# Four one-bank output tiles, a reopened PSUM pool, a last pair combined early, and a remade order

## The chip, the cores and the metric

The kernel runs on one core of one Trainium2 chip. The metric is the device time of one execution in microseconds, as the median of several runs. The core's engines work side by side, each through its own list of instructions in order: TensorE (PE) multiplies matrices and writes PSUM, VectorE (DVE) and ScalarE (ACT) work element by element and empty PSUM, GpSimd (POOL) works element by element on SBUF, and SyncE (SP) issues the DMA transfers. An instruction that has to wait for another engine holds everything behind it on its own engine.

## What is computed

The reference is two softmax attentions in a row and then a feed-forward network with a GELU:

```python
def sm_attn(qq, kk, vv):
    s = scale * np.matmul(qq, kk.transpose(0, 1, 3, 2))
    s = s - np.max(s, axis=-1, keepdims=True)
    a = np.exp(s)
    a = a / (np.sum(a, axis=-1, keepdims=True) + 1e-09)
    return np.matmul(a, vv)
p_packed = sm_attn(p, k, v)            # 32 packed queries per head
attn = sm_attn(q, p_packed, p_packed)  # 576 queries per head
x = attn.transpose(0, 2, 1, 3).reshape(8 * 576, 512)
h = x @ w_in                           # 512 x 2048
g = 0.5 * h * (1.0 + erf(h / np.sqrt(2.0)))
out = g @ w_out                        # 2048 x 512
```

q, k and v have 8 batches, 8 heads, 576 positions and 64 columns a head; everything is float32. `x @ w_in` is regrouped: the second attention's weights times (packed p times w_in), so PE first makes `wps`, the product of the packed values and a block of w_in.

## The kernel before

**Tiling.** The 8 batches are taken in 4 pairs of batches, and d_ff in 4 blocks of 512. A pair and a block make a unit, so there are 16 units, 0 to 15, and a pair is four of them. A unit has 8 `h` products on PE (line 1627, 12 matmuls each; line 1618 is the plain form of the first ones), each followed by a GELU on ACT into SBUF (lines 1652 and 1659). Float32 operands are split in a high part (a cast on ACT) and a low part (the rest, by a subtraction), and a product is three matmuls, high by high, high by low and low by high.

**Pair 0, units 0 to 3.** The output product is the plain one: lines 1689 to 1691 are the three matmuls of one 128-token tile, 128 by 512 outputs, one PSUM bank. Four such banks are filled side by side while four blocks of 128 of d_ff pass, then each is emptied: copied by ACT in the pair's first unit (line 1924), added to an accumulator by DVE in the other three (line 1929). The four banks are the halves of two PSUM tiles of two banks each, `oh_0` and `oh_1`. Waits are kept by tile. A ninth, narrower row of tokens goes through `o_edge` in another pool.

**Pairs 1 to 3, units 4 to 15.** The output product is a 2 by 2 block product with seven products in place of eight, taken in the order `MIXED = ("a22", "a11", "s2", "s3", "s1", "s4", "a12")`. Each is done in two halves of 12 matmuls (line 1811); a half fills one of the tiles `oh_0` and `oh_1`. Before it, sums of GELU blocks are made on POOL (lines 1736 and 1741), the high part on ACT (line 1767) and the low part on DVE (line 1773). After it, the half is copied (ACT, line 1836) or added on DVE (line 1842) into an accumulator in SBUF: m4, c11, c12, u3 or c22. The products in `CHAIN` add up in PSUM, each with the one before, without giving the tile back. At the end of a pair three additions on POOL (line 1858) combine accumulators: u3 goes into m4, then u3 and c22 go into c12. Then DVE turns blocks back (line 1899) and SP stores them (line 1890). In unit 15 the low parts of `LAST_LOW = (2, 4)`, which are s2 and s1, are made by POOL.

**Beside all that** run the loads of q, k, v and the weights, the two attentions of the coming pair (k and q are turned by DVE, line 848, or by PE, line 859), the decoding of the weights (lines 1402 to 1465 on ACT, DVE and POOL; the values pass through DRAM in blocks `wf`, `wx`, `ws`), and `wps` (line 1544, made ready by line 1555 on ACT and line 1560 on DVE). In the first 53 us, before the first output product, PE gets filler matmuls on a zero tile (line 1598) wherever the planner sees it with nothing to do; their number is fixed when the kernel is built.

**What sets the order.** Every operation is created by a small task (a generator that yields operations and events). A dry run numbers them; the table `TURNS` (line 118) then lists, for each engine and for the DMA queue, these numbers in the order in which the instructions are issued. The planner walks through the table with modelled costs (`LATENCY`, the `DMA_...` constants; `MARGIN` is added before a PE operation that is neither an `h` product nor an output product, after the first output product; `DMA_MARGIN` before a DMA). These costs set no wait on the chip. SBUF and PSUM slots are handed out from lists of named owners.

Of the kernel before, what the change touches and what calls it, by code (L numbers as in the profile page):

```python
# [42 lines left out]
DMA_FIRST, DMA_ISSUE, DMA_START, DMA_END, DMA_RATE = 2.5, 0.5, 0.6, 0.9, 390e3  # L43
# [12 lines left out]
LAST_LOW = (2, 4)  # L56
CHAIN = ("a11", "s2", "s3", "s1")
INTO = {"a22": "m4", "a11": "c11", "s2": "c12", "s3": "u3", "s1": "c22", "s4": "c12", "a12": "c11"}

MARGIN = 2.0  # L60

DMA_MARGIN = 1.0
# [536 lines left out]
def packed_attention_gelu_ffn(ctx: ExitStack, tc: tile.TileContext, q, k, v, p, w_in, w_out, out):  # L599
# [51 lines left out]
    def plan(order):  # L651
# [1129 lines left out]
        def load_one(u, m):  # L1781
# [3 lines left out]
                [(wms, f"wm_{u}_{m}")])  # L1785
            fire(wm_ready[u, m])

        def mixed_steps():
            for u in range(NF, NU):
                chain = {}  # L1790
                for m, name in enumerate(MIXED):
# [35 lines left out]
        def evict(u, m, h, t):  # L1827
# [18 lines left out]
            if m < 5:  # L1846
                fire(added[u, name, h])
# [177 lines left out]
```

## Time and profile before

| | |
|---|---|
| median of three runs | 724.3 us (723.17 to 725.18) |
| the profiled execution | 725.19 us, of which the span is 723.4 us |
| PE busy | 693.1 us, 96% of the span, 5987 matmuls |
| DVE busy | 537.7 us, 74% |
| ACT busy | 394.7 us, 55% |
| POOL busy | 292.1 us, 40% |
| PE waiting for L1929 or L1924 at L1689 | 3.4 us in 3 waits, 0.9 us in 1 |

The profile is of one execution. Its span runs from the first to the last instruction; 1.8 us of its time lie outside. PE's list of busy time leaves 30.3 us of the span; the weight loads (PEld) run beside the matmuls. In the lines that follow a row begins with its start or its source line, then engine and operation, then output<-input by tile name; `memory` is the one large SBUF tile in which most buffers lie, `rounded` the one for the high and low parts, and `oh` stands for both two-bank tiles and the halves. An arrow in square brackets gives the engine's idle time just before, and what ended it.

### The profile page before, as it was taken

What the parts mean: (1) busy time and instruction counts of PE and PEld (TensorE: products, weight loads), DVE (VectorE), ACT (ScalarE), POOL (GpSimd) and SP (SyncE); (2) the same over time, 40 slices, a digit from 0 to 9 for tenths busy, and PEclk for the clock granted to TensorE, in tenths of its full rate; (3) what the DMA queues carried; (4) which work ended last, traced back from release to release, by engine and by line L of the source; (5) the groups of instructions that cost most, each with busy time, mean ns of one, the idle gap of its engine ahead of it and who ended that gap; (6) DMA issues with size and microseconds to landing.
All of it is one profiled execution on the core that took longest, in us unless ns stands there. A gap on an engine that the chain in (4) does not pass through costs nothing.

```text
span 723.4 us, 14766 instructions
## 1 busy us (share of the span) xinstructions
PE 693.1 (96%) x5987; PEld 611.2 (84%) x5987; DVE 537.7 (74%) x695; ACT 394.7 (55%) x596; POOL 292.1 (40%) x201
## 2 busy tenths in 40 slices
PE   7899999999899999999999999999999999999982
PEld 6667778786786997898899998998998999999982
DVE  4879889877788827789898766787898835765673
ACT  4778677756565663484654363574645463434320
POOL 2654952574351444123044621232143614142481
PEclk9999999999999999999999999999999999999998
DMA  9877999998575899999225299997723574424226
GB/s 327 256 234 196 261 258 241 227 312 222 205 234 190 249 263 274 214 189 321 95 88 175 90 211 219 171 233 204 202 88 146 133 219 126 147 93 144 90 89 127
DMA packets 199555, 140.42 MB, mean 194 GB/s; under 512 B 153792, under 2 KB 172224, under 8 KB 199488
## 3 DMA queue, kind: packets, MB, share of 16 engines
q1 hardware_dynamic: 199488, 139.49, 70.7%
q8 instruction: 47, 0.77, 0.5%
q14 instruction: 20, 0.16, 0.1%
HBM read 106.95 MB, written 32.51 MB: 193 GB/s over the span
## 4 chain that ended last, share of the span: by engine, by line
PE 77%; DVE 7%; DMA 6%; SPq 3%; ACT 3%; issue 1%; POOL 1%; POOLq 0%; DVEq 0%; ACTq 0%
PE oh L1811 34%; PE h L1627 23%; PE wps L1544 3%; PE oh L1689 3%; PE oh L1691 3%; PE oh L1690 3%; PE s L939 2%; PE oh L1598 1%; PE pp L1130 1%; DMA memory<-in_k_dram 1%; DMA memory<-in_q_dram 1%; DMA out_dram<-memory 1%; SPq L826 1%; POOL memory L1858 1%; DVE memory L1929 1%
## 5 line engine op out<-in xcount | busy, mean ns | idle before, releaser
L1811 PE MATMUL oh<-rounded 128*128 128x288 f32 x2016 | 293.3, 298 | 6.7 <-DVE memory L1842 3.3
L1811 PEld LDWEIGHTS oh<-rounded 128*128 128x128 f32 x2016 | 275.4, 196 | 26.5 <-issue 11.6
L1627 PE MATMUL h<-a2T,wp 128*128 128x288 f32 x1440 | 209.7, 295 | 0.2 <-DVE wp L1560 0.2
L1627 PEld LDWEIGHTS h<-a2T,wp 128*128 128x128 f32 x1440 | 197.6, 188 | 5.1 <-ACT rounded L1767 1.3
L1736 POOL TENSOR_TENSOR memory<-memory 128x1152 f32<-128x1152 f32 x36 | 100.5, 2791 | 147.6 <-ACT memory L1652 90.4
L1773 DVE TENSOR_TENSOR rounded<-memory,rounded 128x1152 fp32r<-128x1152 f32 x82 | 132.3, 1618 | 30.0 <-ACT rounded L1767 29.9
L1842 DVE TENSOR_TENSOR memory<-oh,memory 128x576 f32<-128x576 f32 x138 | 102.5, 749 | 61.0 <-PE oh L1811 50.7
L1767 ACT CAST rounded<-memory 128x1152 fp32r<-128x1152 f32 x84 | 96.8, 1159 | 48.0 <-POOL memory L1736 32.5
L1652 ACT ACTIVATE memory<-h 128x576 f32<-128x576 f32 x96 | 62.4, 653 | 98.4 <-PE h L1627 90.2
L1741 POOL TENSOR_TENSOR memory<-memory 128x1152 f32<-128x1152 f32 x12 | 32.5, 2705 | 148.8 <-ACT memory L1652 132.9
L1689 PE MATMUL oh<-rounded 128*128 128x512 f32 x128 | 53.3, 416 | 4.4 <-DVE memory L1929 3.4
L1691 PE MATMUL oh<-rounded 128*128 128x512 f32 x128 | 50.2, 392 | 0.0
L1690 PE MATMUL oh<-rounded 128*128 128x512 f32 x128 | 50.1, 392 | 0.0
L1560 DVE TENSOR_TENSOR wp<-wps,wp 128x1024 fp32r<-128x1024 f32 x30 | 36.6, 1220 | 16.7 <-ACT wp L1555 16.5
L1555 ACT CAST wp<-wps 128x1024 fp32r<-128x1024 f32 x30 | 30.3, 1015 | 24.4 <-PE wps L1544 24.4
L848 DVE STREAM_TRANSPOSE memory<-memory 128x1152 f32<-128x1152 f32 x24 | 32.7, 1366 | 13.3 <-DMA memory<-in_k_dram 13.3
L1668 DVE TENSOR_TENSOR rounded<-memory,rounded 128x512 fp32r<-128x512 f32 x32 | 28.0, 874 | 15.2 <-ACT rounded L1666 15.2
L1689 PEld LDWEIGHTS oh<-rounded 128*128 128x128 f32 x128 | 24.1, 188 | 17.1 <-DVE memory L1929 5.0
L1659 ACT ACTIVATE memory<-h 128x576 f32<-128x576 f32 x32 | 20.9, 652 | 31.7 <-PE h L1627 24.6
L1451 POOL TENSOR_TENSOR memory<-memory 128x512 int32<-128x512 int32 x16 | 23.4, 1464 | 29.3 <-DVE memory L1431 26.7
L1544 PE MATMUL wps<-memory,pp 64*32 64x512 f32 (+1 forms) x528 | 34.0, 579 | 0.0
L1459 POOL TENSOR_TENSOR memory<-memory 128x512 int32<-128x512 int32 x16 | 21.1, 1319 | 29.7 <-DVE memory L1431 29.7
(144 smaller groups left out, 819.6 us busy)
## 6 DMA issues: line engine op xcount, KB each, us to landing
rounded<-wx SPq DMA_DIRECT2D x84, 512.0 KB, 4.3
memory<-ws SPq DMA_DIRECT2D x24, 512.0 KB, 4.9
wraws<-in_moe_w_out_dram SPq DMA_DIRECT2D x16, 512.0 KB, 5.1
wx<-memory SPq DMA_DIRECT2D x16, 512.0 KB, 4.7
memory<-in_v_dram SPq DMA_DIRECT2D x15, 512.0 KB, 7.0
memory<-in_k_dram SPq DMA_DIRECT2D x48, 144.0 KB, 5.2
memory<-in_q_dram SPq DMA_DIRECT2D x48, 144.0 KB, 5.1
out_dram<-memory SPq DMA_DIRECT2D x48, 144.0 KB, 3.7
```

Of the source, the lines that this page charges most:

```text
L1544: nc.tensor.matmul(t[r0:r0 + 32, hh, :m], lhsT=pp[b][rows, hh, r0:r0 + 32], rhs=wi[u, hh][rows, g, cols], start=True, stop=True)
L1560: yield Op(DVE, 1.22, step, lambda: nc.vector.tensor_tensor(lo, x, hi.bitcast(F32), ALU.subtract))
L1627: nc.tensor.matmul(t[:, half, :HALF], lhsT=w[:, wpart, ch, fc], rhs=a2T[b, ch][:, apart, half * HALF:(half + 1) * HALF], start=ch == 0 and ...
L1652: lambda: nc.scalar.activation(x[:, c % 2].rearrange("p (a n) -> p a n", a=2), t[:, :, :HALF], AF.Gelu), table="gelu")
L1689: nc.tensor.matmul(t, lhsT=g[0], rhs=w[:, 0], start=first, stop=False)
L1690: nc.tensor.matmul(t, lhsT=g[0], rhs=w[:, 1], start=False, stop=False)
L1691: nc.tensor.matmul(t, lhsT=g[1], rhs=w[:, 0], start=False, stop=last)
L1736: return Op(POOL, 2.69, 0, lambda: nc.gpsimd.tensor_tensor(of(x), of(y), of(z), op))
L1767: o = op[u, m] = yield Op(ACT, 1.17, 0, lambda o: nc.scalar.copy(o[:, 0], x), [(ops, f"op_{u}_{m}")])
L1773: engine, cost, 0, lambda: on(engine).tensor_tensor(o[:, 1], x, o[:, 0].bitcast(F32), ALU.subtract), port=True)
L1811: nc.tensor.matmul(t[:, half, :HALF], lhsT=x[:, wpart], rhs=o[:, part, q, half * HALF:(half + 1) * HALF], start=first and q == 0 and wpart ...
L1842: yield Op(DVE, 0.75, 0, lambda: nc.vector.tensor_tensor(to(), x, to(), ALU.add))
```

## The change

Four things are changed.

1. The two two-bank tiles are replaced by four one-bank tiles `o_0` to `o_3` for pair 0. When all of pair 0's banks have been emptied, the pool is closed, and a pool with two two-bank tiles `m_0` and `m_1` is opened in the same banks; the first product of unit 4 is created only then.
2. `LAST_LOW` is (5, 6): in unit 15 the low parts of s4 and a12 are POOL's, and those of s2 and s1 DVE's.
3. For the last pair, the combining additions move ahead. The sums of units 12 to 14 are combined on DVE (three additions on 128 by 1152 elements), while unit 14's last and unit 15's first products run. Unit 15's own products then go straight into the final accumulators: s3 is added to m4 and subtracted from c12, which makes two additions per half in place of one, and s4 joins the PSUM chain (`LAST_CHAIN`) behind s1. Every result is turned back when its last addition is done.
4. `TURNS` is new for all engines, `DMA_END` goes from 0.9 to 1.4, `MARGIN` from 2.0 to 0, `DMA_MARGIN` from 1.0 to 0. PE's last `h` product now stands ahead of nine product halves, before of twelve; the last load of q for pair 0 stands ahead of a v load and of weight loads that it followed before. The table now has 11 more fillers (162, before 151). Everything else is issued as often as before, save three POOL additions that are now DVE's and the two more additions from s3.

```diff
-DMA_FIRST, DMA_ISSUE, DMA_START, DMA_END, DMA_RATE = 2.5, 0.5, 0.6, 0.9, 390e3
+DMA_FIRST, DMA_ISSUE, DMA_START, DMA_END, DMA_RATE = 2.5, 0.5, 0.6, 1.4, 390e3
...
-LAST_LOW = (2, 4)
+LAST_LOW = (5, 6)
 CHAIN = ("a11", "s2", "s3", "s1")
+LAST_CHAIN = CHAIN + ("s4",)
...
-MARGIN = 2.0
-
-DMA_MARGIN = 1.0
+LAST_INTO = {
+    "a22": (("m4", ALU.subtract),), "a11": (("c11", ALU.add),), "s2": (("c12", ALU.add),),
+    "s3": (("m4", ALU.add), ("c12", ALU.subtract)), "s1": (("c22", ALU.add),),
+    "s4": (("c12", ALU.add),), "a12": (("c11", ALU.add),),
+}
+
+MARGIN = 0.0
+
+DMA_MARGIN = 0.0
...
-        "53 62 64 63 56 57 83 61 81 82 80 113 100 68 94 101 71 118 97 119 93 85 72 96 73 139 92 157 110 114 175 "
+        "62 63 53 64 56 57 82 83 80 61 97 101 96 100 114 68 120 81 86 119 93 71 94 73 72 95 135 146 121 123 169 "
...
-    pairs = [ps_o.tile([P, 2, 512], F32, name=f"oh_{i}") for i in range(2)]
+    banks, twos = [ps.tile([P, 512], F32, name=f"o_{i}") for i in range(4)], []
+
+    def two_banks():
+
+        ps_o.close()
+        ps = ctx.enter_context(tc.tile_pool(name="ps_m", bufs=1, space=PSUM))
+        twos.extend(ps.tile([P, 2, 512], F32, name=f"m_{i}") for i in range(2))
...
         def mixed_steps():
+            for i in (0, 1, 2, 3, 5, 6, 7, 8):
+                yield finished[NF - 1, i]
+            if order.dry:
+                yield finished[NF - 1, 4]
+            if not order.dry:
+                two_banks()
             for u in range(NF, NU):
-                chain = {}
+                chain, names = {}, LAST_CHAIN if u == NU - 1 else CHAIN
...
-            if f == 0 and m < 5:
+            if u == NU - 1:
+                for name, op in LAST_INTO[MIXED[m]]:
+                    if name in merged:
+                        yield merged[name]
+                    yield Op(
+                        DVE, 0.75, 0,
+                        lambda name=name, op=op: nc.vector.tensor_tensor(to(name), to(name), x, op))
+                    if (MIXED[m], name) == ("s3", "m4"):
+                        fire(total[pr, NM])
+            elif f == 0 and m < 5:
...
-            engine, cost = POOL, 2.67
+            engine, cost = (DVE, 1.35) if pr == NP - 1 else (POOL, 2.67)
...
+            if pr == NP - 1:
+                for x in ("a22", "s3", "s2", "s1", "s4"):
+                    if x == "s2":
+                        yield combine("m4", "u3", "m4", ALU.subtract)
+                        fire(merged["m4"])
+                    for h in range(2):
+                        yield evicted[NU - 2, MIXED.index(x), h]
+                yield combine("c12", "c12", "u3", ALU.subtract)
+                macs.give(of("u3"))
+                yield combine("c12", "c12", "c22", ALU.add)
+                fire(merged["c12"])
+                yield from totals("a22")
+                yield total[pr, NM]
+                start(result(pr, 0, 0, "m4"))
...
```

Line numbers move with the insertions: the output product's lines 1689 to 1691 become 1703 to 1705, the additions to accumulators (1929 and 1842) become 1979 and 1871, line 848 becomes 861, the low part (1773) becomes 1787, the combine (1858) becomes 1887, and the additions of unit 15 stand at line 1860.

The remade order is shown at three places. The first is PE at the end of unit 2, around 181 to 186 us of the trace: the last products of the unit's four banks and the next `h` product. `oh_0_81` and `oh_1_82` are the two tiles, `o_0_81` to `o_3_84` the four. Before:

```order
L1689 MATMUL oh_1_82<-rounded_80 128x512
L1690 MATMUL oh_1_82<-rounded_80 128x512
L1691 MATMUL oh_1_82<-rounded_80 128x512
L1689 MATMUL oh_1_82<-rounded_80 128x512
L1690 MATMUL oh_1_82<-rounded_80 128x512
L1691 MATMUL oh_1_82<-rounded_80 128x512
L1152 MATMUL ppTm_3_2113<-ident_71,pn_3_0_2091 128x128
L1152 MATMUL ppTm_3_2113<-ident_71,pn_3_1_2093 128x128
L1689 MATMUL oh_0_81<-rounded_80 128x512
L1690 MATMUL oh_0_81<-rounded_80 128x512
L1691 MATMUL oh_0_81<-rounded_80 128x512
L1627 MATMUL h_24_2122<-a2T_0_0_911,wp_3_0_1941 128x288 x6
```

After:

```order
L1703 MATMUL o_2_83<-rounded_80 128x512
L1704 MATMUL o_2_83<-rounded_80 128x512
L1705 MATMUL o_2_83<-rounded_80 128x512
L1703 MATMUL o_3_84<-rounded_80 128x512
L1704 MATMUL o_3_84<-rounded_80 128x512
L1705 MATMUL o_3_84<-rounded_80 128x512
L1703 MATMUL o_0_81<-rounded_80 128x512
L1704 MATMUL o_0_81<-rounded_80 128x512
L1705 MATMUL o_0_81<-rounded_80 128x512
L1165 MATMUL ppTm_3_2124<-ident_71,pn_3_0_2097 128x128
L1165 MATMUL ppTm_3_2124<-ident_71,pn_3_1_2101 128x128
L1641 MATMUL h_24_2128<-a2T_0_0_920,wp_3_0_1786 128x288 x6
```

The fourth product, into the first half of `oh_0` before, has a tile of its own after, and stands ahead of the two transposes (line 1152, now 1165).

The second place is DVE in unit 4, around 272 to 278 us: low parts, the turning of a block of k that has to be loaded first, and the additions of the first mixed products into their accumulators. Before:

```order
L1773 TENSOR_TENSOR rounded_80<-memory_79,rounded_80 128x1152 x4
L848 STREAM_TRANSPOSE memory_79<-memory_79 128x1152
L1516 TENSOR_TENSOR memory_79<-memory_79 128x512
L1773 TENSOR_TENSOR rounded_80<-memory_79,rounded_80 128x1152
L1842 TENSOR_TENSOR memory_79<-oh_0_81,memory_79 128x576
L1560 TENSOR_TENSOR wp_6_0_2795<-wps_6_0_0_3006,wp_6_0_2795 128x1024
L1842 TENSOR_TENSOR memory_79<-oh_1_82,memory_79 128x576
```

After:

```order
L1787 TENSOR_TENSOR rounded_80<-memory_79,rounded_80 128x1152 x4
L1871 TENSOR_TENSOR memory_79<-m_0_2668,memory_79 128x576
L861 STREAM_TRANSPOSE memory_79<-memory_79 128x1152
L1787 TENSOR_TENSOR rounded_80<-memory_79,rounded_80 128x1152
L1871 TENSOR_TENSOR memory_79<-m_1_2669,memory_79 128x576
L1871 TENSOR_TENSOR memory_79<-m_0_2668,memory_79 128x576
L1529 TENSOR_TENSOR memory_79<-memory_79 128x512
```

A further low part and the addition from the first tile have moved ahead of the turning of k (848, now 861), and the next low part and the addition from the second tile stand behind it.

The third place is DVE in unit 15, over the additions from the tiles of its middle products. Before, the row L1899 is the first turning back of a result:

```order
L1773 TENSOR_TENSOR rounded_80<-memory_79,rounded_80 128x1152
L1842 TENSOR_TENSOR memory_79<-oh_0_81,memory_79 128x576
L1842 TENSOR_TENSOR memory_79<-oh_1_82,memory_79 128x576
L1773 TENSOR_TENSOR rounded_80<-memory_79,rounded_80 128x1152
L1842 TENSOR_TENSOR memory_79<-oh_0_81,memory_79 128x576
L1842 TENSOR_TENSOR memory_79<-oh_1_82,memory_79 128x576
L1842 TENSOR_TENSOR memory_79<-oh_0_81,memory_79 128x576
L1773 TENSOR_TENSOR rounded_80<-memory_79,rounded_80 128x1152
L1899 STREAM_TRANSPOSE memory_79<-memory_79 128x576 x2
L1842 TENSOR_TENSOR memory_79<-oh_1_82,memory_79 128x576
L1842 TENSOR_TENSOR memory_79<-oh_0_81,memory_79 128x576
L1842 TENSOR_TENSOR memory_79<-oh_1_82,memory_79 128x576
```

After, L1860 are the additions of unit 15 and L1887 is the last of the three combining additions:

```order
L1787 TENSOR_TENSOR rounded_80<-memory_79,rounded_80 128x1152
L1860 TENSOR_TENSOR memory_79<-memory_79,m_0_2668 128x576
L1860 TENSOR_TENSOR memory_79<-memory_79,m_1_2669 128x576
L1860 TENSOR_TENSOR memory_79<-memory_79,m_0_2668 128x576
L1787 TENSOR_TENSOR rounded_80<-memory_79,rounded_80 128x1152
L1887 TENSOR_TENSOR memory_79<-memory_79 128x1152
L1860 TENSOR_TENSOR memory_79<-memory_79,m_1_2669 128x576
L1860 TENSOR_TENSOR memory_79<-memory_79,m_0_2668 128x576
L1787 TENSOR_TENSOR rounded_80<-memory_79,rounded_80 128x1152 x2
L1860 TENSOR_TENSOR memory_79<-memory_79,m_1_2669 128x576
L1860 TENSOR_TENSOR memory_79<-memory_79,m_0_2668 128x576 x2
L1860 TENSOR_TENSOR memory_79<-memory_79,m_1_2669 128x576 x2
```

The last combining addition (L1887) has come to DVE, between unit 15's first additions, and the low parts of s3 and s1 (the row x2) stand behind an addition from each tile.

## Rows read from the trace of the kernel before

**Rows 1.** Stretch, length, busy PE, PEld, DVE, ACT, POOL, clock, DMA share, GB/s
```profile
0.00:53.00 53.00, 46.38 (x605) 33.78 (x606) 35.97 (x70) 33.51 (x69) 25.37 (x26) 1.00 0.82 274
...
92.00:270.00 178.00, 173.15 (x1328) 143.80 (x1329) 133.79 (x191) 113.65 (x188) 84.88 (x92) 1.00 0.84 241
270.00:284.00 14.00, 12.29 (x90) 11.23 (x89) 9.17 (x11) 6.52 (x8) 4.13 (x2) 0.88 0.97 265
284.00:690.00 406.00, 405.04 (x3638) 377.01 (x3637) 304.76 (x356) 208.43 (x283) 136.40 (x50) 1.00 0.64 165
690.00:724.00 34.00, 17.69 (x127) 16.66 (x125) 19.12 (x23) 3.48 (x3) 15.17 (x5) 0.90 0.46 101
```

**Rows 2.** What PE waited for, whole span: us, times, longest
```profile
PE oh L1689 <- DVE memory L1929: 3.4, 3, 1.8
...
PE oh L1689 <- ACT memory L1924: 0.9, 1, 0.9
...
PE h L1627 <- DVE wp L1560: 0.2, 1, 0.2
```

**Rows 3.** Timeline at 182 to 186: start, us, what, idle before
```profile
182.37 1.22 DVE L1560 TENSOR_TENSOR wp<-wps,wp 128x1024 fp32r<-128x1024 f32 x1 [0.53 <-ACT wp L1555]
...
184.17 1.28 DVE L1929 TENSOR_TENSOR memory<-oh,memory 128x512 f32<-128x512 f32 x2
...
185.50 0.50 PE L1689 MATMUL oh<-rounded 128*128 128x512 f32 x1 [1.83 <-DVE memory L1929]
```

**Rows 4.** Timeline at 272 to 280, PE and DVE
```profile
272.25 1.75 PE L1811 MATMUL oh<-rounded 128*128 128x288 f32 x12
...
272.78 1.38 DVE L848 STREAM_TRANSPOSE memory<-memory 128x1152 f32<-128x1152 f32 x1 [11.21 <-DMA memory<-in_k_dram]
...
276.72 2.97 PE L1811 MATMUL oh<-rounded 128*128 128x288 f32 x12 [1.71 <-DVE memory L1842]
...
279.49 2.21 PE L1627 MATMUL h<-a2T,wp 128*128 128x288 f32 x12
```

**Rows 5.** Timeline at 31 to 45 of SP's queue, then of PE
```profile
31.18 0.39 SPq L884 DMA_DIRECT2D memory<-in_v_dram  x1
...
34.56 0.35 SPq L1398 DMA_DIRECT2D wraws<-in_moe_w_out_dram  x1
36.05 0.35 SPq L816 DMA_DIRECT2D memory<-in_q_dram  x1
...
41.99 0.74 PE L859 MATMUL qm<-ident,memory 128*128 128x128 f32 x5 [0.15 <-DVE mx L1236]
...
44.06 1.25 PE L1598 MATMUL oh<-still 128*128 128x256 bf16 x10 [0.35 <-ACT pp L1115]
```

**Rows 6.** Timeline of PE from the last h product on
```profile
685.89 1.75 PE L1627 MATMUL h<-a2T,wp 128*128 128x288 f32 x12
...
694.38 3.45 PE L1811 MATMUL oh<-rounded 128*128 128x288 f32 x24 [0.40 <-issue]
698.12 4.99 PE L1811 MATMUL oh<-rounded 128*128 128x288 f32 x36 [0.29 <-issue]
704.71 1.86 PE L1811 MATMUL oh<-rounded 128*128 128x288 f32 x12 [1.59 <-DVE memory L1842]
708.77 3.41 PE L1811 MATMUL oh<-rounded 128*128 128x288 f32 x24 [2.20 <-issue]
```

**Rows 7.** Timeline of the same stretch, POOL and then DVE
```profile
698.77 9.11 POOL L1858 TENSOR_TENSOR memory<-memory 128x1152 f32<-128x1152 f32 x3 [2.63 <-DVE memory L1842]
...
700.66 2.00 DVE L1773 TENSOR_TENSOR rounded<-memory,rounded 128x1152 fp32r<-128x1152 f32 x1
...
707.91 1.42 DVE L1842 TENSOR_TENSOR memory<-oh,memory 128x576 f32<-128x576 f32 x2 [3.26 <-POOL memory L1858]
```

**Rows 8.** Every run of line 1773: ns least, median, most
```profile
L1773 DVE TENSOR_TENSOR rounded<-memory,rounded x82: 1315/1350/3827, 240.6 to 700.7; 128x1152 fp32r<-128x1152 f32 x82
```

**Rows 9.** PE groups, 284 to 690: count, busy us, mean ns
```profile
L1544 PE MATMUL wps<-memory,pp 64*32 64x512 f32 x304 | 20.5, 600 | 0.0
```

More of the change, by code (lines that the diff above doesn't have):

```diff
@@ L616, in packed_attention_gelu_ffn @@
     dram = ctx.enter_context(tc.tile_pool(name="dram", bufs=1, space=bass.MemoryType.DRAM))
-    ps_o = ctx.enter_context(tc.tile_pool(name="ps_o", bufs=1, space=PSUM))
     ps_w = ctx.enter_context(tc.tile_pool(name="ps_w", bufs=2, space=PSUM))
+    ps_o = ExitStack()
+    ps = ps_o.enter_context(tc.tile_pool(name="ps_o", bufs=1, space=PSUM))
     ctx.enter_context(tc.manual_schedule())
@@ L676, in plan @@
         psum_o = of_banks(
-            [(i, i + 1, lambda i=i: pairs[i // 2][:, i % 2]) for i in range(4)], [P, 512], (None, (0, 1, 2, 3)))
-        mps = of_banks([(2 * i, 2 * i + 2, lambda i=i: pairs[i][:]) for i in range(2)], [P, 2, 512], (None, (0, 1)), rank=1)
+            [(i, i + 1, lambda i=i: banks[i]) for i in range(4)], [P, 512], (None, (0, 1, 2, 3)))
+        mps = of_banks([(2 * i, 2 * i + 2, lambda i=i: twos[i]) for i in range(2)], [P, 2, 512], (None, (0, 1)), rank=1)
         wide = ring("wide", 2, [P, 2, 512], pool=ps_w)
@@ L1584, in plan @@
         ended = [Event(4) for _ in range(NP)]
-        total = {(pr, m): Event(2) for pr in range(1, NP) for m in range(NM)}
+        total = {(pr, m): Event(2) for pr in range(1, NP) for m in range(NM + 1)}
         added = {(u, x, h): Event() for u in later_units for x in INTO.values() for h in range(2)}
         mixed_up = [Event() for _ in range(NP)]
+        merged = {x: Event() for x in ("m4", "c12")}
         g_ready = [Event() for _ in range(NU * 8)]
@@ L1801, in mixed_steps @@
                     o, w = op[u, m], wm[u, m]
-                    first = name not in CHAIN[1:]
+                    first = name not in names[1:]
                     for h in range(2):
@@ L1829, in evict, with to @@
             x, name = t[:, :, :HALF], INTO[MIXED[m]]
-            def to():
+            def to(name=name):
                 return mac[pr, name][:, h].rearrange("p (a n) -> p a n", a=2)
-            if f == 0 and m < 5:
+            if u == NU - 1:
[8 more added lines that the diff above has]
+            elif f == 0 and m < 5:
                 mac[pr, name] = yield from one(macs, f"mac_{pr}_{name}", ACT, 0)
@@ L1842, in evict @@
                 yield Op(DVE, 0.75, 0, lambda: nc.vector.tensor_tensor(to(), x, to(), ALU.add))
-            if MIXED[m] not in CHAIN[:-1]:
+            if MIXED[m] not in (LAST_CHAIN if u == NU - 1 else CHAIN)[:-1]:
                 mps.give(t)
             fire(evicted[u, m, h])
-            if m < 5:
+            if m < 5 and u < NU - 1:
                 fire(added[u, name, h])
@@ L1862, in totals @@
                     yield total[pr, MIXED.index(name)]
+            if pr == NP - 1:
[12 more added lines that the diff above has]
+                start(result(pr, 0, 0, "m4"))
+                yield from totals("s1")
+                start(result(pr, 0, 1, "c22"))
+                yield from totals("s2", "s3", "s4")
+                start(result(pr, 1, 1, "c12"))
+                yield from totals("a11", "a12")
+                start(result(pr, 1, 0, "c11"))
+                return
             yield from totals("a22", "s3")
```

200 rows, old and new, of the table TURNS are left out of this document.

## The prediction

> **What bounds the kernel now.** I read the engines' busy time by stretch first, then PE's waits over the whole span, then the timeline at each place where PE stood still. The stretches [rows 1] show PE as the bound: from 284 to 690 us it is busy 405.04 of 406 us, so nothing is to be had there unless PE gets less work, and it gets the same. What PE leaves lies in four places: 53.00 − 46.38 = 6.6 us before the first output product, 178.00 − 173.15 = 4.9 in pair 0, 1.7 at 272 to 284 (with a granted clock of 0.88), and a tail in which PE has 17.69 us of work in 34. The list of waits [rows 2] says which lines: 3.4 us for DVE and 0.9 us for ACT in front of pair 0's output products, against 0.2 for the weights of an h product.
>
> **Four one-bank tiles.** At 185.50 PE has waited 1.83 us with the last product of unit 2, into the first half of oh_0 [rows 3]. What ends the wait is the second of two additions of line 1929 that start at 184.17; by the order before, the second half of oh_0 was filled first and is emptied while the first half still has its last product to come. Nothing reads the bank that PE wants to write: the wait is the tile's, and four tiles do away with it. The other waits at this line have the same shape: 3.4 + 0.9 = 4.3 us in four of them. DVE was late there because line 1560 (1.22 us) and a reduction stood ahead of the additions. What may be late next is the same addition from its own bank, when the next unit begins 1.8 us sooner; but the additions behind it stand in DVE's queue behind a low part that waits for a GELU, so they come sooner with PE. I take −3.8, bounds 0 and −4.4. Opening the new pool puts a copy or an addition of each bank ahead of unit 4's first product; its four product halves now stand closer together on PE, so a half may wait for its tile for up to one group, 1.75 us in the first of [rows 4]. Bounds 0 and +1.7, taken +0.8.
>
> **The turning of k.** In unit 4 DVE stands 11.21 us at line 848 for a DMA that lands at 272.78, and low parts and additions are queued behind it [rows 4]. PE waits 1.71 us at 276.72, and the clock falls: 12 mixed matmuls take 2.97 us there and 1.75 at 272.25, 12 h matmuls 2.21 and 1.75 [rows 4, 6]. That is 1.71 + 1.22 + 0.46 = 3.4 us. The new order puts the low part and the addition that PE waits for ahead of line 848. The addition from the second tile still stands behind it, so part of the wait can come back. I take −2.5, bounds 0 and −3.9 (a further 0.5 if the shorter queue also spares the next groups).
>
> **The tail.** After the last h product, at 685.89, PE has twelve product groups and stands 0.40 + 0.29 + 1.59 + 2.20 = 4.5 us [rows 6]. The two long waits come behind DVE, which waits 3.26 us for POOL's three combining additions, 9.11 us in all [rows 7]. The change takes these from POOL and puts them earlier, on DVE, over accumulators that are final before unit 15's own parts: three additions that on DVE have the shape of a low part, 1.35 us alone [rows 8] and 2.00 beside POOL [rows 7], and two more additions of half 1.42 = 0.71 us each [rows 7], so 5.5 to 7.4 us more for DVE. From 690 to 724 DVE is busy 19.12 of 34 us [rows 1], so it has room; and two of the three combining additions stand in unit 14 or before unit 15's first addition. Only nine groups follow the last h product now, since that product moves three groups back; the sum on PE is the same. What is late next is an addition queued behind two low parts in a row (2 × 1.35 to 2 × 2.00 us against a group of 1.75), and POOL's low parts of s4 and a12, which come last. Behind PE's end the additions, the turning and the store stay as they are. I take −4.3, all but 0.2 of the idle time shown; bounds −5.5 (the 4.5 and the slower clock of 0.90 at the end) and −1.0 (two low parts held as below, and the rest lost behind additions).
>
> Here a rule of the Trainium skill bears. The row shows low parts of 1.35 us in the median and 3.83 at most [rows 8], and 2.00 while POOL combines [rows 7]: contended, but not by one whole POOL instruction, which is 9.11 / 3 = 3.04 us. The Trainium skill (SBUF — State Buffer, Who interferes with whom) says that a VectorE instruction with two SBUF inputs shares a port pair with GpSimd as an exclusive lock, so that the loser waits out the other's whole instruction. By the median the rule costs nothing, by the greatest row it holds nearly in full; the rival below prices that.
>
> **The first stage.** The last q load leaves SP's queue at 36.05, behind a weight load that was let go at 34.56, and the transposes that use q run at 41.99 [rows 5]. The new order has this q load ahead of the v load that left at 31.18, so up to 36.05 − 31.18 = 4.9 us sooner, if its slot is free; other chains (keys, softmax, weights) end near the same time, so little of it need reach the first output product. Against it stand 11 more fillers, at 1.25 us for ten [rows 5] some 1.4 us where PE isn't idle. I take −1.0, bounds −4.9 and +1.4.
>
> **Less slack in the order.** With the margins at 0 the table may put PE's short attention steps where their inputs only just arrive, and PE holds all behind them. The trace of before has one such wait of 0.2 us in the rows [rows 2]. Most of the order from 284 to 690 is as it was, with swaps of neighbours. I take +1.5, bounds 0 and +4.
>
> **Sum.** −3.8 + 0.8 − 2.5 − 4.3 − 1.0 + 1.5 = −9.3 us on the profiled execution's 725.19 gives 715.9. This execution lies 0.9 above the median of 724.3, so against the median: 715.0.
>
> **Rivals.**
>
> *Decoding bounds pair 0.* DVE is busy 133.79 of 178 us there and POOL 84.88 [rows 1], and the decoding of weights goes over both. If PE runs 3 us sooner and the decoded weights don't, PE waits for them. For it: DVE's 75%. Against it: the only such wait now is 0.2 us at line 1560's output [rows 2]. It takes back 3 of the 3.8 us: 718.
>
> *The waits change their owner.* The bank itself is late instead of its neighbour, and unit 4 pays the full 1.7 us for the new pool: half of 3.8 and 0.9 more, so 715.0 + 1.9 + 0.9 = 717.8. For it: DVE has additions behind other work, as in rows 3. Then this part of the change doesn't do what it says.
>
> *The port takes the tail.* DVE's combining additions and its low parts of s2 and s1 lie beside POOL's sums and low parts. If two of them are held as in the longest row, 2 × (3.83 − 1.35) = 5.0 us, the tail gains nothing: 719.5. By the row of 2.00 us this is not the usual case. By the rule of the Trainium skill above it would be.
>
> *Slower: PE's queue without slack.* The place is 284 to 690, where there are 304 wps matmuls in groups of 16, 19 groups [rows 9], and as many other attention steps again. Were each of the 38 late by 0.35 us, 13.3 us would come in place of 1.5: 715.0 + 11.8 = 726.8. It decides from about 0.27 us a step on, where the gain of 9.3 us is gone. For it: the margin was 2 us, and DVE is busy 304.76 of 406. Against: the stretch leaves PE 1 us idle now, and a step late by little is covered by PE's products only if they stand ahead of it.
>
> **Chances.** Forecast 0.60, with 711 to 718 as its own range; decoding 0.10; waits that change their owner 0.08; port 0.10; slower 0.12. A measurement of this kernel tells about 0.3%, 2.2 us, from no change. The first four cases lie below 722.1 but for their upper ends, from which, and from the slower rival's lower end, comes a chance of 0.07 for no change: faster 0.82, same 0.07, slower 0.11. The range runs from 709.5 (the first stage and the tail near their bounds) to 722 (the port with the order's +4).
>
> **What would show it.** After: no wait at the output products for an addition or a copy (4.3 us now), or a short one from the same bank; line 861 with a shorter wait of the engines behind it and a clock of 1.0 from 270 to 284; PE idle under 1 us from the last h product on, no wait of DVE for POOL, combines of 1.35 to 2.0 us on DVE; the first output product before 53 us. I am wrong if PE's idle time from 284 to 690 exceeds some 5 us, if the tail from the last h product to the end is as long as the 37 us of before, or if the first stage grows.

## The result: 707.6 us, and the profile after

The changed kernel takes 707.59 us (median of 4 runs, 706.2 to 708.56) against 724.34 (723.17 to 725.18): a ratio of 0.977, 95% interval 0.975 to 0.979. That is 16.75 us less; 9.3 were forecast, and 707.6 lies below the range. The profiled execution took 707.41 us with a span of 705.6, against 725.19 and 723.4 before, so 17.8 us of span are to be accounted for.

Busy time by stretch in the changed kernel; the columns and stretches are those of [rows 1], and the last stretch holds only 4.3 us of PE because PE ends at 694.3:

```profile
0.00:53.00 53.00, 51.80 (x638) 39.82 (x639) 35.69 (x77) 37.82 (x77) 27.81 (x30) 1.00 0.86 280
...
92.00:270.00 178.00, 177.46 (x1394) 149.61 (x1393) 139.07 (x194) 115.10 (x187) 82.69 (x92) 1.00 0.87 250
270.00:284.00 14.00, 14.00 (x137) 12.20 (x137) 12.07 (x13) 6.57 (x11) 7.83 (x3) 1.00 1.01 220
284.00:690.00 406.00, 403.48 (x3591) 377.36 (x3590) 311.79 (x365) 205.41 (x277) 135.10 (x48) 1.00 0.60 162
690.00:724.00 34.00, 4.33 (x33) 4.10 (x32) 5.57 (x8) 0.00 (x0) 0.58 (x1) 0.88 0.36 70
```

Against [rows 1] PE is busy 51.80 us of the first 53 instead of 46.38, leaves 0.5 us of 92 to 270 instead of 4.9, and none of 270 to 284; from 284 to 690 it leaves 2.5 instead of 1.0. The stretches are fixed in time, so the work that falls into them is not quite the same.

What PE waited for in the changed kernel, the whole list; [rows 2] are three rows of the longer one before:

```profile
PE h L1641 <- DVE wp L1573: 1.3, 2, 0.9
PE m L1831 <- DVE rounded L1787: 1.2, 1, 1.2
PE o L1612 <- DVE still L630: 1.0, 1, 1.0
PE m L1831 <- DVE memory L861: 0.5, 1, 0.5
PE o L1705 <- DVE rounded L1682: 0.4, 1, 0.4
```

No output product waits for an addition any more, and no transpose of the first stage for a load. Of the rest, 1.0 us is the start of the first filler, as before. Three waits are new: the two for wp, at 318.95 and 554.09, and one in front of a mixed product, the second of these two rows:

```profile
262.33 1.83 PE L1831 MATMUL m<-rounded 128*128 128x288 f32 x12 [0.54 <-DVE memory L861]
```
```profile
428.65 1.83 PE L1831 MATMUL m<-rounded 128*128 128x288 f32 x12 [1.23 <-DVE rounded L1787]
```

The first row is the product that waited 1.71 us before [rows 4]; the profile puts its wait down to the turning of k. The wait of the second row stands at the same product in all five profiles of the new order (1.10 to 1.71 us; the other four put it down to the load of the operand's weights, `rounded<-wx`) and in none of the nine of the old order.

The tail of the changed kernel, PE's rows from the last hidden product on and POOL's last; they answer to [rows 6] and [rows 7]:

```profile
677.94 1.75 PE L1641 MATMUL h<-a2T,wp 128*128 128x288 f32 x12
679.53 14.80 PE L1831 MATMUL m<-rounded 128*128 128x288 f32 x108
```
```profile
680.46 3.51 POOL L1750 TENSOR_TENSOR memory<-memory 128x1152 f32<-128x1152 f32 x1 [7.01 <-ACT memory L1666]
685.24 5.33 POOL L1787 TENSOR_TENSOR rounded<-memory,rounded 128x1152 fp32r<-128x1152 f32 x2 [1.27 <-ACT rounded L1781]
```

PE runs nine groups, 108 matmuls, without a gap, and POOL no longer combines.

To compare kernels place by place I took from PE's timeline the start of hidden products h_0, h_8, h_48 and h_124 (48.17, 87.67, 298.20 and 673.19 us before), PE's end (712.18) and the span. The table gives the length of each stretch before, and for every later profile the difference from it. Part of a difference is one execution's own: the four profiles that leave the first stage as it was start h_0 between 48.05 and 48.94.

| kernel | to h_0 | h_0 to h_8 | h_8 to h_48 | h_48 to h_124 | to PE's end | rest |
|---|---|---|---|---|---|---|
| before, us | 48.2 | 39.5 | 210.5 | 375.0 | 39.0 | 11.2 |
| changed | −4.5 | −0.2 | −11.0 | +2.9 | −5.1 | +0.1 |
| changed, again | −4.6 | −0.2 | −10.9 | +2.7 | −5.0 | +0.2 |
| tiles_only | −3.3 | −1.0 | −8.1 | 0.0 | 0.0 | −0.1 |
| order_two_tiles | −1.3 | −0.1 | −9.6 | +2.7 | −5.1 | −0.1 |
| tail_only | −0.1 | −0.1 | −2.3 | +3.1 | −5.2 | +0.5 |
| tail2 | +0.3 | 0.0 | −1.8 | +0.1 | −5.0 | −0.2 |
| k_later | +0.8 | 0.0 | −3.3 | +1.7 | 0.0 | −0.2 |
| fillers_wide | −1.4 | −0.6 | −2.1 | +1.2 | 0.0 | −0.2 |
| tiles_wide | −4.1 | −0.5 | −7.0 | +3.1 | 0.0 | −0.1 |
| tiles_tail | −3.5 | −1.0 | −6.4 | +1.2 | −5.1 | −0.1 |
| tiles_tail_more | −3.2 | −1.0 | −6.6 | +3.4 | −5.0 | 0.0 |
| wp_first | −3.8 | −0.2 | −11.1 | +1.3 | −5.0 | +0.1 |
| wp_first_more | −4.0 | −0.2 | −11.1 | +1.4 | −5.1 | 0.0 |

### The profile page after: what moved, and what is told of

It reads as the page before. It is cut to its first block, busy times and chain, and to the rows that moved or that the text cites. A ratio compares the mean times of both kernels' runs of the same rounds, so it can differ in the third digit from the quotient of the medians.

```text
span 705.6 us, 14827 instructions
## 1 busy us (share of the span) xinstructions
PE 689.7 (98%) x5998; PEld 612.7 (87%) x5998; DVE 533.9 (76%) x700; ACT 393.3 (56%) x596; POOL 280.7 (40%) x198
## 4 chain that ended last, share of the span: by engine, by line
PE 88%; DVE 5%; DMA 3%; SPq 2%; issue 1%; ACT 1%; DVEq 0%; ACTq 0%
PE m L1831 33%; PE h L1641 25%; PE wps L1557 4%; PE o L1703 4%; PE o L1705 4%; PE o L1704 4%; PE o L1612 3%; PE s L952 2%; PE h L1632 1%; DMA memory<-in_k_dram 1%; PE pp L1143 1%; SPq L839 1%; DMA rounded<-wx 1%; DVE memory L861 1%; PE o L872 1%
## 5 line engine op out<-in xcount | busy, mean ns | idle before, releaser
L1831 PE MATMUL m<-rounded 128*128 128x288 f32 x2016 | 290.5, 297 | 1.8 <-DVE rounded L1787 1.2
L1831 PEld LDWEIGHTS m<-rounded 128*128 128x128 f32 x2016 | 274.6, 196 | 18.0 <-DVE memory L1871 6.0
L1750 POOL TENSOR_TENSOR memory<-memory 128x1152 f32<-128x1152 f32 x36 | 100.4, 2790 | 148.7 <-ACT memory L1666 89.4
L1871 DVE TENSOR_TENSOR memory<-m,memory 128x576 f32<-128x576 f32 x124 | 91.7, 747 | 62.9 <-PE m L1831 54.4
L1755 POOL TENSOR_TENSOR memory<-memory 128x1152 f32<-128x1152 f32 x12 | 34.4, 2868 | 140.7 <-ACT memory L1666 110.7
L1703 PE MATMUL o<-rounded 128*128 128x512 f32 x128 | 52.9, 413 | 0.0
L1705 PE MATMUL o<-rounded 128*128 128x512 f32 x128 | 50.3, 393 | 0.4 <-DVE rounded L1682 0.4
L1704 PE MATMUL o<-rounded 128*128 128x512 f32 x128 | 50.1, 391 | 0.0
L1682 DVE TENSOR_TENSOR rounded<-memory,rounded 128x512 fp32r<-128x512 f32 x32 | 30.9, 964 | 14.4 <-ACT rounded L1680 14.3
L1557 PE MATMUL wps<-memory,pp 64*32 64x512 f32 (+1 forms) x544 | 35.5, 574 | 0.0
L1703 PEld LDWEIGHTS o<-rounded 128*128 128x128 f32 x128 | 24.1, 188 | 11.0 <-issue 6.5
L1472 POOL TENSOR_TENSOR memory<-memory 128x512 int32<-128x512 int32 x16 | 21.8, 1361 | 28.6 <-DVE memory L1444 26.4
L1865 ACT COPY memory<-m 128x576 f32<-128x576 f32 x30 | 19.2, 642 | 21.2 <-PE m L1831 20.9
```

Of the source, the lines that this page charges most:

```text
L1557: nc.tensor.matmul(t[r0:r0 + 32, hh, :m], lhsT=pp[b][rows, hh, r0:r0 + 32], rhs=wi[u, hh][rows, g, cols], start=True, stop=True)
L1703: nc.tensor.matmul(t, lhsT=g[0], rhs=w[:, 0], start=first, stop=False)
L1704: nc.tensor.matmul(t, lhsT=g[0], rhs=w[:, 1], start=False, stop=False)
L1705: nc.tensor.matmul(t, lhsT=g[1], rhs=w[:, 0], start=False, stop=last)
L1750: return Op(POOL, 2.69, 0, lambda: nc.gpsimd.tensor_tensor(of(x), of(y), of(z), op))
L1831: nc.tensor.matmul(t[:, half, :HALF], lhsT=x[:, wpart], rhs=o[:, part, q, half * HALF:(half + 1) * HALF], start=first and q == 0 and wpart ...
```

## The experiments

**The four tiles alone (tiles_only), and the rest without them (order_two_tiles).** The first is the kernel before with this edit and its own order; the second is the changed kernel with the edit undone.

```diff
-    pairs = [ps_o.tile([P, 2, 512], F32, name=f"oh_{i}") for i in range(2)]
+    banks, twos = [ps.tile([P, 512], F32, name=f"o_{i}") for i in range(4)], []
+    def two_banks():
+        ps_o.close()
+        ps = ctx.enter_context(tc.tile_pool(name="ps_m", bufs=1, space=PSUM))
+        twos.extend(ps.tile([P, 2, 512], F32, name=f"m_{i}") for i in range(2))
```

> The kernel before, order and all, with four one-bank tiles for pair 0 and the pool reopened ahead of unit 4. Theory A (a tile's other half makes PE wait wherever a two-bank tile is written: in front of pair 0's output products, 4.4 us, and for the fillers and small products of the first stage, 2 us or more): 715 to 718 us. Rival B (the first stage was shortened by the order alone, the q and k loads standing earlier): only pair 0's 4.4 us go, 719.9 us, and the first output product stays at 53.3 us. Rival C (the waits pass to the bank's own addition): 722 us or more.

> The changed kernel, its order and its last pair, with the two two-bank tiles of before. Theory A: pair 0's waits come back (4.4 us or somewhat more, since this order was made for four tiles) and 2 us or more in the first stage: 714 to 717 us. Rival B: only pair 0's come back, 712 us, the first output product stays at 50 us. Rival C: under 710 us.

Measured: tiles_only 714.21 us, ratio 0.989 (0.984 to 0.993); order_two_tiles 711.3 us, ratio 0.983 (0.980 to 0.987). The tiles by themselves bring 1.1% (0.7 to 1.6), more than I gave them, and by the table 3.3 of their 12.4 us lie in the first stage. order_two_tiles fits neither of its theories: the first stage's 3.2 us came back (−1.3 against −4.5), but from h_8 to h_48 only 1.4. PE's waits in its first 54 us, for tiles_only and then for order_two_tiles:

```profile
PE o L1609 <- DVE still L628: 1.0, 1, 1.0
PE o L1609 <- ACT e1T L1075: 0.9, 1, 0.9
PE km L870 <- DMA memory<-in_k_dram: 0.8, 1, 0.8
```
```profile
...
PE oh L1610 <- DVE memory L877: 0.7, 1, 0.7
PE oh L1610 <- DVE mx L1019: 0.6, 1, 0.6
PE oh L1610 <- ACT memory L877: 0.6, 1, 0.6
PE oh L1610 <- ACT pn L1115: 0.5, 1, 0.5
PE oh L1610 <- ACT pp L1126: 0.4, 1, 0.4
...
```

With two-bank tiles a filler that writes one half waits for whoever reads the other, five times in these rows; with four tiles in the same order, the changed kernel, none is left. On the order of before there were four such waits, and tiles_only has one. From h_8 to h_48 the two parts don't add: tiles alone give −8.1 us, the order alone −9.6, both −11.0. The order also takes most waits from that stretch by itself: PE's idle time there is 7.7 us before, 3.0 in tiles_only, 1.9 in order_two_tiles and 0.5 in the changed kernel. And the new pool has a price in tiles_only. Its first mixed product, on PE, and DVE ahead of it:

```profile
234.22 3.44 PE L1828 MATMUL m<-rounded 128*128 128x288 f32 x24 [1.12 <-DVE memory L1946]
```
```profile
230.82 2.75 DVE L1784 TENSOR_TENSOR rounded<-memory,rounded 128x1152 fp32r<-128x1152 f32 x1 [0.70 <-ACT rounded L1778]
233.49 0.68 DVE L1946 TENSOR_TENSOR memory<-o,memory 128x512 f32<-128x512 f32 x1
```

The last addition from an old bank stands behind a low part of 2.75 us, and the reopened pool lets no product begin before it: 1.12 us. In the changed kernel all additions stand ahead of that low part, and the product waits for nothing.

SP's queue in tiles_only, whose instructions stand there in the order of before: the weight load that was let go at 34.56 and the last q load that left at 36.05 [rows 5] now read

```profile
31.22 0.35 SPq L1409 DMA_DIRECT2D wraws<-in_moe_w_out_dram  x1
32.54 0.35 SPq L827 DMA_DIRECT2D memory<-in_q_dram  x1
```

The load is 3.5 us sooner though nothing was moved in the queue: what PE does late in the first stage comes back to it as a late load. This holds beyond one execution: the four profiles with two tiles and the order and fillers of before let it go at 35.7 to 36.5, the four with four tiles on that order at 32.5 to 33.2. PE's wait of 1.2 us for q went with it.

**Which instructions were held: fillers off the output banks, with two tiles (fillers_wide) and with four (tiles_wide).**

```diff
-            for r in (psum_o, wide):
+            for r in (wide,):
```

> The kernel before, whose fillers of the first 53 us no longer write the two-bank tiles: they take a tile of the wide pool or are left out. Theory A: fillers that wait for a reader of the other half of their tile hold PE, and through it the decoding and SP's queue; without them most of the 3.3 us of the four tiles in that stretch comes: 721 us (719.5 to 722.5), first hidden product at 44.8 to 46.5 us. Rival B: the small products themselves wait for the other half, and the fillers only stand in the gaps: 724 us (723 to 725), first hidden product at 47.5 to 48.5. Rival C: with fewer fillers the granted clock of the first stretch falls below 0.9 and small products take longer: 726 us or more.

> The four one-bank tiles on the order of before (tiles_only), whose fillers take the wide pool alone, as in fillers_wide. It tells how much of the first stage's 3.3 us was the fillers' and how much the small products' own. Theory: with four tiles neither fillers nor small products wait for another bank's reader, so the fillers are worth nothing either way: first hidden product at 44.3 to 45.3, 714.2 us (713 to 715.5); then of the 3.34 us the fillers held 1.4 (fillers_wide) and the small products 1.9. Rival: without the fillers in the output banks the granted clock of the first stage falls below 0.97 or PE's gaps lengthen, first hidden product at 46 or later, 716 us or more.

Measured: fillers_wide 724.65 us, ratio 1.000 (0.997 to 1.003); tiles_wide 716.79 us, ratio 0.991 (0.988 to 0.994). The whole times hide the answer, since both give back 1 to 3 us after h_48, where no filler runs; the first column of the table holds it. With two tiles, taking the fillers off the output banks brings h_0 forward by 1.4 us, although one of them now waits 1.3 us for a reader of its wide tile; then making the tiles four brings 2.7 more (46.74 to 44.03). So the greater part seems to be the small products' own waits, and neither theory A nor B holds alone. PE's waits in the first 54 us of fillers_wide show them, at the transposes and products of attention themselves:

```profile
PE oh L1097 <- ACT e1T L1064: 0.9, 2, 0.5
...
PE oh L939 <- DVE memory L1177: 0.7, 1, 0.7
PE oh L859 <- ACT e1T L1057: 0.6, 1, 0.6
...
```

PE ran 567 matmuls instead of 605 in its first 53 us there, at a granted clock of 1.00: rival C is refuted. The 716.79 us of tiles_wide is its rival's number, but h_0 stands at 44.03, where the rival said 46 or later. With four tiles, h_0 is 0.8 us earlier without fillers on the output banks (44.83 against 44.03); that is within the 0.9 us by which profiles of one order differ, so it is not shown that they cost anything.

**The turning of k (k_later).** VectorE's order before, with one instruction moved:

```diff
-transposed(k, batch 4)
 low part (4,6)
 evict(4,5,h0)
+transposed(k, batch 4)
```

> The kernel before with one DVE instruction moved: the turning of the first block of k for batch 4 stands behind the low part of a12 and the first addition of s4 in unit 4, before ahead of them. Theory: the 1.7 us wait at 276.7 and the half clock behind it (another 1.7 us) go: 720.9 us, clock 1.0 from 270 to 284. Rival (the wait comes back at the next addition, which still stands behind the turning): 723 us or more and the clock still falls.

Measured: 724.36 us, ratio 1.001 (0.999 to 1.004). No gain: my step falls. The stretch h_8 to h_48 is 3.3 us shorter than in the profile before, but so it is by 1.8 to 2.3 us in tail_only, tail2 and fillers_wide, which leave this place as it was. In the profile of k_later the wait at this product and the fall of the clock are gone, and yet the whole time is no shorter, since only one of eight profiles of the old order has them so long: in the seven others DVE stands 7.8 to 10.3 us for the load of k, but PE waits at this product between nothing and 0.8 us, and the clock stays at 1.00. The 1.71 us of [rows 4] with the clock behind them were that one execution's.

**The combined tail alone (tail_only, tail2).** The constants and functions of the last pair, with the changed kernel's order for units 14 and 15 behind the order of before. In tail2 one of VectorE's instructions at the seam stands three places later.

```diff
-LAST_LOW = (2, 4)
+LAST_LOW = (5, 6)
+LAST_CHAIN = CHAIN + ("s4",)
+    "s3": (("m4", ALU.add), ("c12", ALU.subtract)), "s1": (("c22", ALU.add),),
```

> The kernel before with the last pair's part alone: LAST_CHAIN, LAST_INTO, LAST_LOW (5, 6), the combining additions on DVE ahead, and the changed order from unit 14's later products on. Theory: the tail from h product 124 to PE's end falls from 39.0 to about 34 us by itself: 719.2 us. Rival (the gain is the order's from earlier on, or DVE's additions only trade with POOL's): 722 us or more.

> The kernel before with the last pair's combined accumulators alone, and now with VectorE's order of before kept up to the end of low(14,0), so that the wait of 1.58 us at 665.71 which the earlier piece (tail_only) brought at its seam should not arise. Theory: the tail alone is worth the 5.1 us that PE lost in its last stretch, so 719.3 us (718.2 to 720.5), ratio about 0.993. Rival: the work that the combining moves forward meets other waits before the end and gives back half of it, so 721.5 us (720.5 to 723) as tail_only showed.

Measured: tail_only 721.96 us, ratio 0.998 (0.996 to 1.000); tail2 720.12 us, ratio 0.994 (0.991 to 0.997). Both have the full 5 us in the last stretch of PE. In tail_only my seam gave a part back:

```profile
665.71 1.86 PE L1823 MATMUL oh<-rounded 128*128 128x288 f32 x12 [1.58 <-DVE memory L1863]
```

In tail2 that is gone, and the stretch before the tail is +0.1. The tail is worth 5.0 to 5.2 us by its stretch, and 4.7 by the whole times of tail2 (724.83 to 720.12 on its chip).

**Tiles and tail on the old order (tiles_tail, tiles_tail_more), beside the changed kernel (again).** The two edits above together; their second run shares its chip with the changed kernel.

> The four one-bank tiles, the reopened pool and the combined tail together, on the order of before. Theory: the two parts act in stretches that do not touch (the first 250 us, the last 40 us), so they add: 714.2 - 4.9 = 709.3 us (708.3 to 710.8), and what the remade order of the changed kernel is worth beyond them is 709.3 - 707.6 = 1.7 us. Rival: the order is what makes the tail pay, so 712 us (711 to 714).

> The changed kernel itself, unaltered, on the chip of the three below, so that differences of a few tenths of a per cent between them can be read. Every theory: 707.6 us (706 to 709).

> The four tiles and the combined tail on the order of before (tiles_tail) once more, beside the changed kernel on the same chip. Theory: the remade order is worth nothing beyond the two parts, within 1 us of the changed kernel. Rival: it is worth the 1.7 us by which the sum of the parts (709.3) missed 707.6, so 1.2 to 2.2 us above the changed kernel.

Measured: tiles_tail 708.6 us, ratio 0.977 (0.973 to 0.980). On the second chip again 707.26, ratio 0.978 (0.976 to 0.980), and tiles_tail_more 711.39, ratio 0.984 (0.981 to 0.986). There the remade order is worth 4.1 us beyond the two parts, more than either expectation gave it. The two runs of one kernel disagree; their profiles differ by 2.5 us of span, 2.3 of them between h_48 and h_124, where the slower one has

```profile
299.68 1.20 PE L957 MATMUL s<-memory,pT 64*32 64x288 f32 x32 [1.41 <-ACT memory L1671]
...
429.91 3.43 PE L1836 MATMUL m<-rounded 128*128 128x288 f32 x24 [1.41 <-ACT memory L1870]
```

and the faster only 0.98 us at the second place. In both profiles the order's advantage from h_8 to h_48 is the same, 4.3 to 4.6 us. How much of it lasts to the end is not settled: near nothing by the ratio of the first run, 0.977 like the changed kernel's (the two did not run on one chip there), 4 us on the chip that ran both.

**The two new waits for wp (wp_first, wp_first_more).** VectorE's order in the changed kernel, at two places:

```diff
-mixed_weight(4, f3)
 evict(6,0,h0)
 wp low part (unit 7, j1)
+mixed_weight(4, f3)
...
-low part (11,6)
 wp low part (unit 13, j0)
+low part (11,6)
```

> The changed kernel with two places of VectorE's order exchanged: the low part of wp stands ahead of the mixed weight (314.35) and ahead of the low part of (11,6) (549.56), the two that lengthened to 2.75 and 3.35 us beside GpSimd and let PE wait 0.89 and 0.41 us. Theory: both waits go and nothing takes their place, 706.3 us (705.5 to 707.0). Rival: what is moved behind is late in its turn, or the lengthening meets another instruction that PE waits for: 707.6 us or more.

> The changed kernel with the two exchanges in VectorE's order (wp_first) once more, with more rounds and beside the changed kernel. Theory: the two waits of 0.89 and 0.41 us are gone and nothing replaces them, so 1.3 us below the changed kernel. Rival: the load of a mixed operand that PE met 1.48 us late at 428.26 is what comes in their place, and the gain is under 0.5 us.

The first place in the changed kernel, with POOL, DVE, ACT and PE in order of time, and then in wp_first_more:

```profile
313.90 2.65 POOL L1750 TENSOR_TENSOR memory<-memory 128x1152 f32<-128x1152 f32 x1 [4.55 <-DVE rounded L1787]
...
314.35 2.75 DVE L1529 TENSOR_TENSOR memory<-memory 128x512 fp32r<-128x512 f32 x1
314.53 1.01 ACT L1568 CAST wp<-wps 128x1024 fp32r<-128x1024 f32 x1 [2.01 <-PE wps L1557]
...
317.69 1.21 DVE L1573 TENSOR_TENSOR wp<-wps,wp 128x1024 fp32r<-128x1024 f32 x1
...
318.95 1.86 PE L1641 MATMUL h<-a2T,wp 128*128 128x288 f32 x12 [0.89 <-DVE wp L1573]
```
```profile
316.01 1.23 DVE L1578 TENSOR_TENSOR wp<-wps,wp 128x1024 fp32r<-128x1024 f32 x1 [0.49 <-ACT wp L1573]
...
317.15 0.68 DVE L1534 TENSOR_TENSOR memory<-memory 128x512 fp32r<-128x512 f32 x1
...
318.25 1.82 PE L1646 MATMUL h<-a2T,wp 128*128 128x288 f32 x12
```

The mixed weight's low part, started 0.45 us after the start of a POOL addition, lasts 2.75 us; started after the addition's end, 0.68. PE's wait is gone, and so is the other. What PE still waits for after h_48 is the mixed product of the third new wait, 1.71 us here. Measured: wp_first 705.8 us, ratio 0.973 (0.969 to 0.977); wp_first_more 706.16 (705.0 to 706.57) beside the changed kernel's 707.26 (705.37 to 709.15) on the same chip, ratios 0.976 (0.974 to 0.978) and 0.978 (0.976 to 0.980). The profiles say 1.3 us less from h_48 to h_124; the times lean the same way by 1.1 us, but their intervals overlap. The 705.8 us are the lowest of all medians, but no version is shown to be faster than the changed kernel.

## Why the prediction was wrong

The direction and the places were right: four output banks, the tail, and PE's idle time as what there is to win. The signs that the prediction named came too: the first output product at 50.07, the clock at 1.00 from 270 to 284, 2.5 us of idle time from 284 to 690, no gap behind the last h product. The sum failed on one step outright, the first stage, where the two-bank tile was not priced at all, and on sizes from h_8 to h_48. By stretches, forecast against measured on the profiled executions (−9.3 and −17.8):

- **The first stage**, the step that failed outright: "I take −1.0", measured −4.5 and −4.6 to h_0 (−3.2 to the first output product, ahead of which the new order has one more h product). I followed one late load and argued that other chains end near the same time. Much of their lateness had one cause, which I had priced in pair 0 only: in the first stage the same two-bank tiles carry the transposes, the small products and the fillers, and each of these waited for a reader of the other half. PE stood idle 6.1 us ahead of h_0 before, 2.8 in tiles_only, 1.2 in the changed kernel. tiles_only gives −3.3 of it without touching the order, of which fillers_wide can account for 1.4; the order alone gives −1.3. The 11 more fillers, for which I set 1.4 against it, cost at most 0.5 us: PE's busy time up to h_0 went from 42.0 to 42.5.
- **Four tiles in pair 0**: "−3.8, bounds 0 and −4.4". All the waits of [rows 2] at line 1689 went, 4.3 us, in the changed kernel and in tiles_only. In the changed kernel 0.5 us for the edge product and 0.7 us for a transpose went too, which I left out; these are the order's, since tiles_only still has them (0.5 and 1.1). **The new pool**, "+0.8, bounds 0 and +1.7", costs 1.12 us on the old order (tiles_only; 1.11 in tiles_tail_more) and nothing on the new one, where the additions come in time: the wait was priced rightly for the old order, and I missed that the new one puts the additions ahead of the low part.
- **The turning of k**: "−2.5" has no support. k_later, which does just that, gains nothing, and three kernels with the old order there are 1.8 to 2.3 us shorter from h_8 to h_48 than the profile before. I took a wait seen in one execution for a property of the order. What stood in its place: from h_8 to h_48 I forecast −3.8 + 0.8 − 2.5 = −5.5 and found −11.0. Of these, 7.2 are PE's idle time (7.7 to 0.5) and 1.7 the slower clock of before; 2.1 are in no wait that the profile lists. By the three kernels above some 2 of the 11.0 were the profiled execution's own misfortune, so some 9 are the change's, an estimate; the tiles alone give −8.1 and the order alone −9.6 in that same stretch.
- **The tail**: "−4.3, bounds −5.5 and −1.0", measured −5.1, and tail2 shows it by itself at −5.0. Mechanism right; PE's 4.5 us of idle time went whole, and 0.6 more that no listed wait holds. The additions behind two low parts did not come late.
- **Less slack**: "+1.5, bounds 0 and +4", measured +2.9 and +2.7: inside the bounds, but not at the attention steps that I named. PE's idle time from h_48 to h_124 in the changed kernel is 2.5 us, and all of it lies in the three new waits, which come with the new order: 1.3 at two h products for wp, gone in wp_first_more, and 1.2 at one mixed product for its operand, which wp_first_more keeps in its +1.4. Kernels with the old order have 0.0 to +3.4 there by waits at other products, so the whole is no more than single executions of the old order lose there.

The rivals: decoding did not bound pair 0 (no wait for wp before 318.95), no wait changed its owner, and none of the slower rival's 38 steps shows a wait in the list after. The port did not take the tail: PE has no gap there. But the lock that this rival rests on is real, as below.

The sum of the parts is the last point. Each against the kernel before on its own chip, tiles_only takes off 9.0 us (723.17 to 714.21) and tail2 4.7; with between 0 and 4.1 for the order that makes 13.7 to 17.8, which holds the 16.75 measured. What remains open is the order's share: without the four tiles it takes off 11.9 together with the tail (order_two_tiles), since order and tiles remove in part the same waits.

## What to carry to other kernels

A buffer that two users share by halves, where waits are kept by tile, makes every user of one half wait for the readers of the other: list all who use such a tile, in every stage, before pricing the split, since the waits are short, spread over many lines, and come back as late loads. Before a stall in a profile is counted as a gain, ask whether the order or that one execution made it; a load's arrival is of the second kind until another execution shows it. Where no later wait is in sight, give a removed wait its whole length, as the tail shows (4.5 us of idle time, 5.0 to 5.2 gained), and look at stretches, not at whole times, when parts of a few us are compared.

## What the runs showed of the hardware

**VectorE waits out GpSimd's instruction.** Three of DVE's long instructions in the changed kernel, each beside POOL. The one at the wp place above: POOL ends at 316.55, DVE's at 317.10, 0.55 us later, of the 0.68 that it takes alone. The two others, low parts of 1.35 us in the median:

```profile
418.61 2.67 POOL L1755 TENSOR_TENSOR memory<-memory 128x1152 f32<-128x1152 f32 x1 [9.84 <-DVE rounded L1787]
```
```profile
418.70 3.79 DVE L1787 TENSOR_TENSOR rounded<-memory,rounded 128x1152 fp32r<-128x1152 f32 x1 [0.23 <-ACT rounded L1781]
...
549.56 3.35 DVE L1787 TENSOR_TENSOR rounded<-memory,rounded 128x1152 fp32r<-128x1152 f32 x1
```

The first ends 1.21 us behind POOL's end at 421.28; the second, 1.22 us behind the last of three POOL additions, which ended at 551.69. So DVE does nearly its whole work after POOL is done. All 82 low parts of 128 by 1152 in the changed kernel's trace say the same: the 22 that start while a POOL instruction runs end 1.21 to 1.30 us after that instruction's end, whether 0.06 or 2.62 us of it were left; the other 60 take 1.31 to 1.36 us, also where a POOL instruction starts beside them. The rule of the Trainium skill that the prediction weighed (SBUF — State Buffer, Who interferes with whom), an exclusive lock that the loser waits out, agrees with these rows. My reading of it from the median was too weak: what decides is whether POOL's instruction has already begun. The 2.00 us of [rows 7], from which I took that a whole POOL instruction is not waited out, are such a case: that low part starts 0.78 us before the end of the first of the three POOL additions and ends 1.21 us after it.

**Halves of one tile, and banks.** The Trainium skill (PSUM — Partial Sum Buffer, Summary: rules for kernel authors) advises that what is read while a matmul runs be a different bank from the one it writes, or at least a different quadrant, guarded by bank. The halves were such banks all along, and PE waited: 4.3 us at the output products [rows 2]. The wait was for the tile. With each bank a tile of its own, none of these waits is in the list after, nor in that of tiles_only, which keeps the order of before.

**A wait and the clock behind it.** Of the 14 profiles, two show a granted clock below 1.00 in the middle of the program, each right behind a PE wait of 1.7 to 1.8 us: the one before [rows 4], and tail2, whose clock is 0.66 from 185 to 190 us, at

```profile
184.92 0.50 PE L1701 MATMUL oh<-rounded 128*128 128x512 f32 x1 [1.82 <-DVE memory L1971]
...
185.72 2.67 PE L1639 MATMUL h<-a2T,wp 128*128 128x288 f32 x12
...
190.23 1.74 PE L1639 MATMUL h<-a2T,wp 128*128 128x288 f32 x12
```

where 12 matmuls take 2.67 us and 1.74 later. The wait of 1.83 us in the profile before [rows 3], at the same product, has no such fall behind it: the clock of its stretch is 1.00 [rows 1]. So the fall does not follow every such wait, and which execution has it is not to be told from the order.
